# Products and last step of a long convolution in three channel parts instead of two, with a normalisation moved from VectorE to GpSimd and a new order table

## The chip, the cores and the metric

The kernel runs on one core of one Trainium2 chip. The time is the device time of the program in microseconds, from the runs of the unchanged kernel 651.96 us (median of three, 651.33 to 653.91). Five engines share the work: TensorE (PE, with its weight loads PEld), VectorE (DVE), ScalarE (ACT), GpSimd (POOL) and SyncE (SP), which here only issues transfers.

## The reference

Two independent layers over 2048 positions and 576 channels; their outputs are set side by side. All values are float32.

```python
# A: a state space layer as a long convolution, one filter K for each channel d
dt = exp(log_dt); A = -exp(log_A_real) + 1j * A_imag; C = (C_real + 1j * C_imag) * dt[:, None]
P = exp((A * dt[:, None])[:, :, None] * arange(L))          # [576, 128, 2048]
K = 2.0 * einsum("dn,dnl->dl", C, P).real                   # [576, 2048]
y = irfft(rfft(u_t, 2 * L) * rfft(K, 2 * L))[:, :, :L] + u * D_skip
# B: linear attention with a softmax feature map, 32 heads of 18 channels
q, k, v = split(x @ wqkv)
phi_q = concat([softmax(q @ w_phi), softmax(-(q @ w_phi))])  # per head
phi_k = concat([softmax(k @ w_phi), softmax(-(k @ w_phi))])
num = phi_q @ (phi_k^T v); den = phi_q . sum(phi_k) + 1e-6
b = (num / den) @ wo
out = concat([a, b], axis=-1)                                # [1, 2048, 1152]
```

## The kernel before

**Layer B** runs in sixteen key tiles and sixteen query tiles of 128 positions. A key tile (`key_tile`) loads x, splits it into a rounded and a rest part (`load_x`: one copy on ACT, two subtractions on POOL, L399), multiplies it by the folded key weights and the value weights, takes both softmaxes (`softmax`) and adds to one accumulated product of keys and values in PSUM. `softmax` takes maxima, minima and differences on DVE, a second difference on POOL, one exponential on ACT (L514), the sums and their reciprocals on DVE (L515, L516), and a product of the 128x1152 exponentials with the reciprocals on the engine that its argument names. For keys this is the constant `KN`, for queries "dve". The query tiles need all keys and the folded query weights, which take the place of the key weights in SBUF. Each query tile ends with its own store.

**Layer A** builds the filter in 36 groups of channels (`phases`, `waves`, `group`): phases on POOL (L793, L797), sines on ACT (L806 to L808), three small matmuls and exponentials in PSUM (L827), four products on DVE (L832 to L837), 32 small matmuls, and a copy to `ks`. Nine groups make a quarter of the channels, q = 0 to 3. At the end of a quarter `k_first` does the first step of its transform and writes it (L857) to `kd`, a scratch tensor in HBM. `u_first` does the same for u in sixteen pieces, and writes `ud` (L667). The transform's second step, the product with the filter and the way back are `product(p, half)`: eight blocks p of frequencies for each half of the channels. Such a unit loads the tables fu and fi (L895), four blocks ub of `ud` (L912), and for two rows r the table fk (L939) and a block kb of `kd` (L941). It runs 16 matmuls on ub, 8 on each kb and 16 back, each in two passes. In between ACT copies four tiles from PSUM to `us` and four to `zo`, DVE makes eight products `ac` and POOL four sums of them. Six stores (L978, L981) put the result into `zd`. Every read of `ud` waits for all of `ud`, every read of a `kd` tensor for all of that tensor; a half's `kd` is two quarters. `last(cb, half)` reads `zd` (L994), does the last step with eight matmuls, and stores half the channels of 256 positions (L1007).

**The order.** Nothing of this order is fixed by the loops. All operations are first collected with `pl.op`, each with an engine, an estimated cost and its operands. `Plan.run` then places them one by one: among the operations of an engine that could start now it takes the one with the smallest rank. The rank is the number that the table `WANT` gives to the unit that the operation belongs to (`pl.at("product", 3)` and so on). The same rank decides who gets a tile's buffers first: for most tiles a unit may not take a buffer ahead of a lower rank if that would leave the lower rank without one. So each engine's order of instructions, and SP's queue with it, comes out of this table and the estimated costs. Where the plan foresees PE waiting, `emit` puts filler matmuls on a tile of zeros (L200) ahead of an operation, so that PE keeps its clock.

Lines that the text names again: L200 the filler matmul, L388 every other matmul (`mm`), L393 and L395 copies, L399 every two-operand elementwise instruction (`tt`), L591 and L618 transposes of queries.

Of the kernel before, what the change touches and what calls it, by code (L numbers as in the profile page):

```python
# [26 lines left out]
HD = D // 2  # L27
BW = D // NB
# [306 lines left out]
def c_dma(nbytes, run=4096):  # L335
# [4 lines left out]
FR, KN = "dve", "dve"  # L340
# [29 lines left out]
def body(tc, nc, i, out, ctx):  # L370
    pl = Plan()
# [12 lines left out]
    tags({1: "gd", 5: "dram"}, space=DRAM)  # L384
# [252 lines left out]
    kd, zd = ([B("dram", [64, 64, HD]) for _ in range(2)] for _ in range(2))  # L637
# [212 lines left out]
    def k_first(qt, ks):  # L850
        def one(j):
# [3 lines left out]
            for c in range(2):  # L855
                b0, c0, d = 16 * j + 8 * c, qt % 2 * 4 * DQ, kd[qt // 2]
                op("sp", c_dma(64 * 4608, 576), lambda c=c, b0=b0, c0=c0, d=d: sp.dma_start(  # L857
                    d.t[:, b0:b0 + 8, c0:c0 + 4 * DQ], o.t[64 * c:64 * c + 64].rearrange("p b f d -> p b (f d)")), r=[o], w=[d])
# [30 lines left out]
    def product(p, half):  # L889

        pl.at("product", 8 * half + p)
        cs = halves[half]
        fu, fi = B("fu", [128, 4, 2, 32]), B("fi", [128, 2, 2, 64])
        for b, n in ((fu, "fu"), (fi, "fi")):
            op("sp", c_dma(128 * 1024, 1024), lambda b=b, n=n: sp.dma_start(b.t.rearrange("p a b c -> p (a b c)"), i[n][p]), r=[ud], w=[b])  # L895

        ub = [B("ub", [128, 2, HD]) for _ in range(2)]
# [6 lines left out]
        def take(par, r):  # L904
            q = 4 * p + 2 * r
            d = lambda: ub[par].t[64 * r:64 * r + 64]
            if par and not q:
                for j in range(2):
                    op("sp", c_dma(64 * 1152, 1152), lambda j=j: sp.dma_start(d()[:, j], block(1, j, ud)[:, cs]), r=[ud], w=[ub[1]])
                return  # L910
            a = 63 - q if par else q
            op("sp", c_dma(64 * 2304, 1152), lambda: sp.dma_start(  # L912
# [8 lines left out]
        us = [B("us2", [128, 2, HD]) for _ in range(2)]  # L921
        pu, begun = [B("ps", [128, HD]) for _ in range(4)], Mark()
# [8 lines left out]
        op("pe", 970, f, r=[fu, *ub], w=[*pu, begun], with_=us, mode=(64, 32))  # L931
        for r in range(2):
            for part in range(2):
                copy("act", lambda r=r, part=part: us[r].t[:, part], lambda r=r, part=part: pu[2 * r + part].t, [pu[2 * r + part]], [us[r]], HD)
        acs = []

        def times(r):
            fk, kb, ac = B("fk", [128, 2, 128]), B("kb", [128, 2, HD]), B("ac", [128, 4, HD])
            op("sp", c_dma(128 * 1024, 1024), lambda: sp.dma_start(fk.t.rearrange("p a b -> p (a b)"), i["fk"][2 * p + r]), r=[ud], w=[fk])  # L939
            blk = lambda: kd[half].t.rearrange("(p j r) b d -> p (r b) j d", j=2, r=2)[2 * p + r]  # L940
            op("sp", c_dma(128 * 2304, 1152), lambda: sp.dma_start(kb.t, blk()), r=[kd[half]], w=[kb])  # L941
            pk = [B("ps", [128, HD]) for _ in range(2)]
# [5 lines left out]
            op("pe", 970, f, r=[fk, kb, begun], w=pk, with_=[ac], mode=(128, 64))  # L948
            for part in range(2):
                for k, q in ((part, part), (2 + part, 1 - part)):  # L950
                    tt("dve", lambda k=k: ac.t[:, k], lambda q=q: us[r].t[:, q], lambda part=part: pk[part].t, ALU.mult, [us[r], pk[part]], [ac], HD)
# [5 lines left out]
            tt(YN[0], lambda: ac.t[:, 0], lambda: ac.t[:, 0], lambda: ac.t[:, 1], ALU.subtract, [ac], [ac], HD)  # L957
            tt(YN[1], lambda: ac.t[:, 2], lambda: ac.t[:, 2], lambda: ac.t[:, 3], ALU.add, [ac], [ac], HD)
# [3 lines left out]
        pz, zo = [B("ps", [128, HD]) for _ in range(4)], [B("zo", [128, 2, HD]) for _ in range(2)]  # L962
# [6 lines left out]
        op("pe", 970, back, r=[fi, *acs], w=pz, with_=zo, mode=(32, 64))  # L969
        for c in range(4):  # L970
            j, par = divmod(c, 2)
            copy("act", lambda c=c, j=j, par=par: zo[par].t[:, j], lambda c=c: pz[c].t, [pz[c]], [zo[par]], HD)

        def put(par, r):
            q = 4 * p + 2 * r
            s = lambda: zo[par].t[64 * r:64 * r + 64]
            if not par:
                op("sp", c_dma(64 * 2304, 1152), lambda: sp.dma_start(zd[half].t[q:q + 2].rearrange("j s d -> s j d"), s()), r=[zo[0]], w=[zd[half]])  # L978
# [57 lines left out]
```

## Time and profile before

| | us |
|---|---|
| median of three runs | 651.96 (651.33 to 653.91) |
| the profiled execution, its own time | 650.51 |
| span of its trace | 648.5 |

The mean granted TensorE clock is 0.982 of full speed. The transfer queue of SP has 101,574 packets, 102.81 MB, whose time is 55.6% of the span of 16 DMA engines. The trace's rows name engine, line, operation, out<-in with the shape, and a count; what follows is said where a row stands. A stage's row gives the time in which an engine was busy, its instructions in brackets, then the granted clock, the DMA share and GB/s. Matmuls are pipelined and their ends are modelled, so that a busy PE is not a PE at its peak, and the fillers count as busy.

### The profile page before, as it was taken

To read this page: it belongs to the slowest core of one execution; us is meant where nothing else is said; L and a number is where in the kernel's file an instruction comes from. 1 tells how busy PE (TensorE), PEld (TensorE's weight loads), DVE (VectorE), ACT (ScalarE), POOL (GpSimd) and SP (SyncE) were. 2 spreads that over 40 slices of the span, in tenths; PEclk is the share of its full clock that TensorE was granted. 3 is DMA by queue.
4 is the path that set the end of the run, shared out by engine and by line. 5 is a ranking of instruction groups with operands and counts; after the bars stand their busy time and mean duration, and the time that the engine had idled before them with its cause. 6 is when DMAs were issued, how large, how long until landed. Compare 5 with 4: busy or idle time off the path is not lost.

```text
span 648.5 us, 19206 instructions
## 1 busy us (share of the span) xinstructions
PE 597.5 (92%) x7782; PEld 468.8 (72%) x7782; DVE 468.5 (72%) x964; ACT 465.3 (72%) x838; POOL 298.3 (46%) x468
## 2 busy tenths in 40 slices
PE   9989999999998958978889999989979999999997
PEld 5878888888887836856666666656767876678885
DVE  6855978998986869964669787476795666657552
ACT  5799786999985968788778886889965354354332
POOL 1794646567724734560736745365301142435110
PEclk9989999999999979999979999898999999999999
DMA  8966432431256112355437866873567788897466
GB/s 220 290 221 197 128 127 76 136 100 47 67 127 171 33 36 75 99 118 187 144 98 194 230 162 188 226 201 81 167 187 183 222 240 221 227 259 182 149 199 203
DMA packets 101661, 104.02 MB, mean 160 GB/s; under 512 B 12358, under 2 KB 90054, under 8 KB 101574
## 3 DMA queue, kind: packets, MB, share of 16 engines
q1 hardware_dynamic: 101574, 102.81, 55.6%
q8 instruction: 61, 1.00, 0.7%
q14 instruction: 26, 0.21, 0.1%
HBM read 63.63 MB, written 39.06 MB: 158 GB/s over the span
## 4 chain that ended last, share of the span: by engine, by line
PE 43%; DVE 24%; ACT 15%; DMA 7%; issue 4%; POOL 4%; SPq 2%; POOLq 0%; ACTq 0%; DVEq 0%
PE ps L388 39%; DVE e L399 4%; DVE cs L832 3%; DVE E L833 3%; DMA xi<-in_xT_dram 2%; DVE small L515 2%; ACT cs L808 2%; ACT cs L806 2%; PE ps L591 2%; DMA ub<-dram 2%; ACT e L514 2%; ACT cs L807 2%; DVE E L835 1%; DVE E L837 1%; DVE small L516 1%
## 5 line engine op out<-in xcount | busy, mean ns | idle before, releaser
L388 PE MATMUL ps<-wh,xl 128*128 128x288 f32 (+2 forms) x448 | 141.2, 315 | 0.0
L388 PE MATMUL ps<-wh,xh 128*128 128x378 f32 (+2 forms) x400 | 134.7, 337 | 2.1 <-DVE E L833 1.1
L388 PE MATMUL ps<-wl,xh 128*128 128x378 f32 (+2 forms) x400 | 129.0, 323 | 0.0
L797 POOL TENSOR_TENSOR cs<-cs,pi 128x512 int32<-128x512 int32 (+4 forms) x180 | 112.7, 630 | 10.1
L388 PEld LDWEIGHTS ps<-wh,xh 128*128 128x128 f32 x400 | 76.0, 190 | 13.5 <-issue 5.2
L388 PEld LDWEIGHTS ps<-wh,xl 128*128 128x128 f32 x448 | 85.0, 190 | 0.5 <-DVE xl L399 0.3
L399 POOL TENSOR_TENSOR xl<-xi,xh 128x512 fp32r<-128x512 f32 x32 | 41.0, 1282 | 82.3 <-ACT xh L393 76.1
L388 PEld LDWEIGHTS ps<-wl,xh 128*128 128x128 f32 x400 | 75.9, 190 | 0.1
L399 POOL TENSOR_TENSOR ac<-ac 128x288 f32<-128x288 f32 x64 | 51.1, 822 | 46.1 <-DVE ac L399 45.0
L399 POOL TENSOR_TENSOR e<-small,e 128x576 f32<-128x576 f32 x32 | 38.3, 1195 | 72.8 <-DVE small L399 72.5
L832 DVE TENSOR_TENSOR cs<-ps,cs 128x1024 f32<-128x1024 f32 x36 | 43.9, 1218 | 25.7 <-ACT ps L827 25.5
L827 ACT ACTIVATE ps<-ps 128x512 f32<-128x512 f32 x108 | 56.4, 584 | 6.2 <-PE ps L388 5.7
L200 PE MATMUL ps<-zero 128*32 128x256 bf16 (+10 forms) x318 | 57.4, 319 | 1.2 <-DVE zero L415 1.2
L388 PE MATMUL ps<-E,cs 128*32 128x64 f32 x2304 | 44.2, 226 | 13.1 <-DVE E L835 9.6
L515 DVE TENSOR_REDUCE small<-e 128x64 f32<-128x1152 f32 x32 | 42.9, 1347 | 17.3 <-ACT e L514 17.2
L399 DVE TENSOR_TENSOR ac<-us,ps 128x288 f32<-128x288 f32 x128 | 48.9, 446 | 7.9 <-PE ps L388 4.2
L388 PEld LDWEIGHTS ps<-E,cs 128*32 128x32 f32 x2304 | 36.3, 113 | 24.4 <-DVE E L835 9.9
L388 PE MATMUL ps<-wh,xi 128*128 128x288 f32 x160 | 49.5, 311 | 1.0 <-DVE cs L832 0.7
L388 PEld LDWEIGHTS ps<-kvb,fT 126*128 126x128 f32 (+1 forms) x320 | 40.0, 195 | 14.0 <-ACT ks L393 4.5
L388 PE MATMUL ps<-kvb,fT 126*128 126x133 f32 (+1 forms) x320 | 42.7, 284 | 7.3 <-ACT ks L393 3.7
L506 DVE TENSOR_REDUCE small<-ps 128x16 f32<-128x288 f32 (+2 forms) x64 | 28.9, 452 | 26.3 <-PE ps L388 26.2
L388 PE MATMUL ps<-wl,xi 128*128 128x288 f32 x160 | 47.0, 295 | 0.0
(130 smaller groups left out, 1297.4 us busy)
## 6 DMA issues: line engine op xcount, KB each, us to landing
xi<-in_xT_dram SPq DMA_DIRECT2D x32, 320.0 KB
dram<-zi SPq DMA_DIRECT2D x16, 576.0 KB
dram<-zi SPq DMA_DIRECT2D x32, 288.0 KB
kb<-dram SPq DMA_DIRECT2D x32, 288.0 KB
zi<-dram SPq DMA_DIRECT2D x16, 576.0 KB
ub<-dram SPq DMA_DIRECT2D x62, 144.0 KB
ub<-in_u_dram SPq DMA_DIRECT2D x16, 288.0 KB
out_dram<-ot SPq DMA_DIRECT2D x16, 288.0 KB
```

What stands on the lines that cost most here:

```text
L200: self.matmul(t[0:cols, 0:n], self.zero.t[0:rows, 0:cols], self.zero.t[0:rows, 0:n])
L388: pe.matmul(o, l, r, start=start, stop=stop, skip_group_check=skip)
L399: op(eng, c_dve(n) if eng == "dve" else c_pool(n), lambda: e.tensor_tensor(dst(), a(), b(), op=alu), r=r, w=w, lock=eng == "pool" or not a ...
L506: op("dve", c_dve(DH * m), lambda: dve.tensor_reduce(mx.t, v(), axis=AX.X, op=ALU.max), r=[p], w=[mx])
L514: op("act", c_act(1152), lambda: act.activation(e.t, e.t, AF.Exp), r=[e], w=[e], table="exp")
L515: op("dve", 1270, lambda: dve.tensor_reduce(sm.t, e.t, axis=AX.X, op=ALU.add), r=[e], w=[sm])
L591: pe.transpose(tp.t[0:m, j - j0, :], e.t[:, sign, 7 * g:7 * g + GRP[g], :].rearrange("p h f -> p (h f)"), ident.t)
L797: op("pool", c_pool(2 * n * W), lambda n=n, j=j: pool.tensor_tensor(x()[:, :, :, n:2 * n], x()[:, :, :, 0:n], pi.t[:, j:j + 2, gs].bitcast ...
L806: act.activation(cs.t[:, 0], cs.t[:, 1].bitcast(I32), AF.Abs)
L827: op("act", c_act(512), lambda p=p: act.activation(p.t, p.t, AF.Exp), r=[p], w=[p], table="exp")
L832: op("dve", c_dve(64 * W), lambda: dve.tensor_tensor(F(), both(M.t), F(), op=ALU.mult), r=[M, cs], w=[cs])
L833: op("dve", c_dve(64 * W), lambda: dve.tensor_tensor(E.t[:, :, :, 32:64], both(up.t), cs.t[:, :, :, 0:32], op=ALU.mult), r=[up, cs], w=[E])
```

## The change

The channels of `product` and `last` are cut at 144 and 288 in place of 288 alone: `PARTS` has a quarter, a quarter and a half. There are three `kd` and three `zd` tensors. The filter's first two quarters each have their own, the last two share one. `product` runs for 24 units instead of 16, the first sixteen of them 144 columns wide. `last` still runs sixteen times with the same bytes; for a quarter part one run covers twice as many positions of half as many columns. The key tiles' normalisation goes from DVE to POOL (`KN`). `WANT` is replaced as a whole, with 24 ranks for `product`. Cut to its core:

```diff
+PARTS = ((0, D // 4), (D // 4, D // 2), (D // 2, D))
...
-FR, KN = "dve", "dve"
+FR, KN = "dve", "pool"
...
-    ident=[-265.4],
-    fold=[-386.9, -94.8, 140, 322.2],
-    start=[-91.6],
-    key=[-167.8, 70.6, 39.4, 134.7, 162.1, 26, -99.8, 92.7, 123.8, 136.5, 127.6, 52.4, 119.4, 85.3, 65.9, 81.6],
-    kv=[-232.9],
-    query=[857, 388.8, 625.9, 167.6, 333.7, 1000.1, 787.3, 438.6, 557.3, 379.6, 436.8, 493.6, 507.5, 170.5, 578,
-          1378.9],
-    u=[27, 41.2, 77.5, 103.4, 46.3, 50.8, 135.8, 91.1, 50, 111.5, 0.9, -22.5, 29.5, -53.6, -50.4, -78.3],
-    mags=[-26.4],
-    sel=[-18.9, 15.8],
-    dsk=[76.9],
-    par=[-542.3, 43.5, 82.6, 297.6, 159.4, 317.7],
-    group=[24.8, -7.3, 62.4, 23.8, 82, 75.2, 75.8, 64.7, 83.4, 149.4, 127.2, 124.6, 147.9, 105.6, 112.1, 89.2, 147.1,
-          147.3, 179.8, 174.3, 180.5, 158, 181.9, 162.3, 168.4, 199.5, 166.2, 403, 297.6, 505, 233.6, 353.9, 201.1,
-          483.7, 226.4, 210.4],
-    kfirst=[81.5, 102.8, 137.8, 237.5],
-    product=[224.1, 180.6, 177.4, 234.3, 183.8, 189.4, 217, 176.6, 337.3, 365.9, 305.8, 697.2, 383.1, 362.5, 442.5,
-          581.6],
-    last=[318.2, 194.4, 220.9, 233.7, 166.3, 179.1, 287.7, 234.6, 346.7, 612, 290.6, 373.2, 597.2, 1060.5, 389.3,
-          788.5],
+    ident=[158.3],
+    fold=[-399.2, -460.7, 208.1, 236.8],
+    start=[154.8],
+    key=[-397.9, 14.5, 186.8, 190.8, 14.1, -46.4, 46.9, 195, 140.8, -36.5, 189.4, 120.4, 27.6, 175.4, -333.1, 50.8],
+    kv=[-36.7],
+    query=[342.6, 1356.4, 1953, 830.4, 304.2, 281.8, 2222.6, 2128.9, 441.3, 305.2, 543.4, 2600.3, 387.2, 215.9, 436.8,
+          1162.7],
+    u=[43.7, -97.4, -36.7, -176.8, 8.4, -139.2, 72, 15.7, 88.3, -52.9, 95.1, 7.5, 25.4, -17.3, -306.4, -239.3],
+    mags=[-513.9],
+    sel=[-289, -179.6],
+    dsk=[-117.5],
+    par=[-1334.4, 78.7, 82.5, 238.7, 321.3, 330.9],
+    group=[-330.7, -34.3, -219, 24.6, -86.4, 29.4, 15.8, 11.2, -21.4, 112.1, 132.4, 87.4, 139.5, 110.1, 142, 116.9,
+          98, 124.6, 189.9, 182.7, 150.3, 191.9, 147.7, 205, 186.6, 171, 207.6, 364.8, 2555.3, 300, 420.5, 272.7,
+          516.6, 224.4, 307.1, 1435.8],
+    kfirst=[65, 107.4, 160.6, 341.3],
+    product=[323.1, 112.1, 99.9, 203.1, 190, 150.3, 357.2, 179, 307.7, 296.6, 335.2, 168.9, 158.7, 1560.5, 140.2, 251,
+          571.8, 401.9, 548.2, 1367.8, 555, 832.4, 590.8, 423.5],
+    last=[265.1, 257.9, 256.3, 373.4, 848.1, 1298.9, 525.5, 1353.4, 2098.2, 1503.9, 1536, 373, 984, 926.9, 1150.5,
+          407.5],
...
-    kd, zd = ([B("dram", [64, 64, HD]) for _ in range(2)] for _ in range(2))
+    kd, zd = ([B("dram", [64, 64, c1 - c0]) for c0, c1 in PARTS] for _ in range(2))
...
-                b0, c0, d = 16 * j + 8 * c, qt % 2 * 4 * DQ, kd[qt // 2]
+                b0, c0, d = 16 * j + 8 * c, max(0, qt - 2) * 4 * DQ, kd[min(qt, 2)]
...
-    def product(p, half):
-        pl.at("product", 8 * half + p)
-        cs = halves[half]
+    def product(p, part_of):
+        pl.at("product", 8 * part_of + p)
+        cs = slice(*PARTS[part_of])
+        wd = cs.stop - cs.start
...
-        op("pe", 970, f, r=[fu, *ub], w=[*pu, begun], with_=us, mode=(64, 32))
+        op("pe", 3.37 * wd + 20, f, r=[fu, *ub], w=[*pu, begun], with_=us, mode=(64, 32))
...
-    def last(cb, half):
-        pl.at("last", 8 * half + cb // 4)
-        yo, zi = B("yo", [128, 2, HD]), B("zi", [128, 4, HD])
+    def last(k, part_of, cb):
+        pl.at("last", k)
+        c0, c1 = PARTS[part_of]
+        n = c1 - c0
+        m = HD // n
+        yo, zi = B("yo", [128, 2, HD]), B("zi", [128, 4 * m, n])
         op("sp", c_dma(128 * 4608), lambda: sp.dma_start(
-            zi.t, zd[half].t.rearrange("q (r b) d -> (q r) b d", r=2)[:, cb:cb + 4]), r=[zd[half]], w=[zi])
+            zi.t, zd[part_of].t.rearrange("q (r b) d -> (q r) b d", r=2)[:, cb:cb + 4 * m]), r=[zd[part_of]], w=[zi])
...
+    k = 0
+    for part_of, (c0, c1) in enumerate(PARTS):
+        m = HD // (c1 - c0)
+        for cb in range(0, 32, 4 * m):
+            last(k, part_of, cb)
+            k += 1
```

The other lines of the diff put the width `wd` in place of 288 in the shapes, costs and transfers of `product`.

More of the change, by code (lines that the diff above doesn't have):

```diff
@@ L383, in body @@
     tags({8: "ps"}, space=PSUM, window=1000)
-    tags({1: "gd", 5: "dram"}, space=DRAM)
+    tags({1: "gd", 7: "dram"}, space=DRAM)
     B, op = pl.buf, pl.op
@@ L920, in place @@
             return 1 - j if par and (p or r) else j
-        us = [B("us2", [128, 2, HD]) for _ in range(2)]
-        pu, begun = [B("ps", [128, HD]) for _ in range(4)], Mark()
+        us = [B("us2", [128, 2, wd]) for _ in range(2)]
+        pu, begun = [B("ps", [128, wd]) for _ in range(4)], Mark()
         def f():
@@ L961, in product @@
             times(r)
-        pz, zo = [B("ps", [128, HD]) for _ in range(4)], [B("zo", [128, 2, HD]) for _ in range(2)]
+        pz, zo = [B("ps", [128, wd]) for _ in range(4)], [B("zo", [128, 2, wd]) for _ in range(2)]
         def back():
@@ L1004, in last @@
             copy("act" if r else "dve", lambda r=r: yo.t[:, r], lambda r=r: ps[r].t, [ps[r]], [yo], HD)
-        for n in range(2):
+        for h in range(2):
             st = out.ap[0][0]
-            op("sp", c_dma(64 * 2304, 1152), lambda n=n: sp.dma_start(bass.AP(
-                tensor=out.tensor, offset=out.offset + (2 * n + cb) * st + HD * half, ap=[[32 * st, 64], [st, 2], [1, HD]]),
-                yo.t[64 * n:64 * n + 64]), r=[yo])
-    for half in range(2):
-        for cb in range(0, 32, 4):
-            last(cb, half)
+            op("sp", c_dma(64 * 2304, 4 * n), lambda h=h: sp.dma_start(bass.AP(
+                tensor=out.tensor, offset=out.offset + (2 * m * h + cb) * st + c0, ap=[[32 * st, 64], [st, 2 * m], [1, n]]),
+                yo.t[64 * h:64 * h + 64].rearrange("p r (b d) -> p (r b) d", b=m)), r=[yo])
+    k = 0
[4 more added lines that the diff above has]
+            k += 1
     with tc.manual_schedule():
```

45 lines of the change are left out of this document (23 added, 22 removed).

## The prediction

> **What bounds the kernel now.** I read the page's head first, then the busy time of the engines in four stages (cut at the first key softmax, the end of the keys, and the two ends of the products), then the filler matmuls in the same stages, then the transfers that open and close each stage.
>
> ```profile
> span 648.5 us, 19206 instructions
> PE 597.5 (92%) x7782; PEld 468.8 (72%) x7782; DVE 468.5 (72%) x964; ACT 465.3 (72%) x838; POOL 298.3 (46%) x468
> PE 43%; DVE 24%; ACT 15%; DMA 7%; issue 4%; POOL 4%; SPq 2%; POOLq 0%; ACTq 0%; DVEq 0%
> ...
> 33.00:200.00 167.00, 162.10 (x2418) 140.72 (x2417) 138.02 (x265) 145.28 (x240) 99.83 (x157) 0.99 0.42 126
> 200.00:300.00 100.00, 81.54 (x1113) 65.45 (x1111) 74.12 (x154) 78.42 (x127) 50.60 (x80) 0.97 0.34 94
> 300.00:505.00 205.00, 186.87 (x2726) 134.49 (x2726) 147.54 (x277) 164.33 (x302) 91.48 (x153) 0.97 0.61 170
> 505.00:648.50 143.50, 135.83 (x1355) 104.75 (x1353) 84.64 (x202) 56.71 (x134) 42.00 (x50) 1.00 0.75 213
> ```
>
> In a stage's row the busy columns are PE, its weight loads, DVE, ACT and POOL; then come granted clock, DMA share and GB/s. PE carries the largest share of the chain of waits and is the fullest engine in every stage. But part of its busy time is filler on zeros, which L200 issues where the plan foresees a gap. The same stages for the zero tile alone (first column again PE):
>
> ```profile
> 200.00:300.00 100.00, 19.29 (x132) 12.96 (x132) 0.00 (x0) 0.97 0.34 94
> 300.00:505.00 205.00, 12.60 (x69) 6.39 (x69) 0.00 (x0) 0.97 0.61 170
> 505.00:648.50 143.50, 11.58 (x54) 5.58 (x54) 0.00 (x0) 1.00 0.75 213
> ```
>
> So PE does nothing useful for 100 − 81.54 + 19.29 = 37.8 us of the 100 us after the keys, for 205 − 186.87 + 12.60 = 30.7 us of the next 205, and for 7.7 + 11.6 = 19.3 us of the last 143.5. Between 33 and 200 us it idles 4.9 us of 167: that stage is full. The hole to look at is 200 to 300 us. What could have been run there shows in the transfers that go through the scratch tensors in HBM:
>
> ```profile
> L981 SPq DMA_DIRECT2D dram<-zo x64: 540/595/1939, 344.4 to 606.0; - x64
> L912 SPq DMA_DIRECT2D ub<-dram x62: 573/610/1699, 314.8 to 582.3; - x62
> L857 SPq DMA_DIRECT2D dram<-zi x32: 574/634/2056, 178.1 to 506.4; - x32
> L941 SPq DMA_DIRECT2D kb<-dram x32: 371/450/1217, 294.9 to 589.3; - x32
> L667 SPq DMA_DIRECT2D dram<-zi x16: 320/327/583, 28.7 to 306.1; - x16
> ```
>
> The first quarter's filter leaves at 178 us (L857, first), but the first product starts at 295 to 315 us (L941, L912): it needs a half, that is two quarters, and also all sixteen pieces of u, whose last is written only at 306 us (L667). The last filter quarter leaves by 506 us, the last product result at 606 us.
>
> **The quarter units: cost of the split.** Eight units of half a width become sixteen of a quarter: the same columns, with twice the instructions. One half unit's matmuls, from the timeline (start, duration; the last row holds both rows r of one kind):
>
> ```profile
> 521.70 1.20 PE L388 MATMUL ps<-ub,fu 64*32 64x288 f32 x32
> 524.88 1.23 PE L388 MATMUL ps<-ac,fi 32*64 32x288 f32 x32
> 526.62 2.16 PE L388 MATMUL ps<-kb,fk 128*64 128x288 f32 x16
> ...
> L388 PE MATMUL ps<-kb,fk 128*64 128x288 f32 x256 | 38.4, 433 | 2.0 <-ACT xi L393 1.1 <-DVE E L833 0.5 <-DMA kb<-dram 0.3
> L591 PE MATMUL ps<-ident,e 128*126 128x128 f32 x128 | 17.8, 279 | 7.0 <-DVE e L399 6.4 <-DVE cs L832 0.6
> ```
>
> A half unit is 1.20 + 1.23 + 2.16 = 4.59 us of PE. No 144-column matmul is in the trace; between the 279 ns of 128 columns and the 433 ns of 288, a straight line gives 279 + 16/160 × 154 = 294 ns, 0.68 of the half's. So I take 0.68 × 4.59 = 3.1 us a quarter unit, 16 × 3.1 = 50 us in place of 8 × 4.59 = 36.7: +13.2 us. The bounds are 0 (time goes with the columns) and +36.7 (a quarter unit as long as a half).
>
> ```profile
> L393 ACT ACTIVATE us<-ps 128x288 f32<-128x288 f32 x64 | 22.3, 418 | 22.5 <-PE ps L388 20.0 <-issue 2.0
> L393 ACT ACTIVATE v<-ps 128x396 f32<-128x396 f32 x16 | 8.1, 506 | 5.0 <-PE ps L388 4.9
> L393 ACT ACTIVATE v<-ps 128x180 f32<-128x180 f32 x16 | 5.2, 325 | 5.3 <-PE ps L388 2.3 <-DVE small L507 1.5 <-DVE small L399 0.9
> L399 DVE TENSOR_TENSOR ac<-us,ps 128x288 f32<-128x288 f32 x128 | 48.9, 446 | 7.9 <-PE ps L388 4.2 <-ACT zo L393 3.5
> L399 DVE TENSOR_TENSOR e<-ps,small 128x198 f32<-128x198 f32 x16 | 5.6, 351 | 0.4 <-ACT v L393 0.4
> L399 POOL TENSOR_TENSOR ac<-ac 128x288 f32<-128x288 f32 x64 | 51.1, 822 | 46.1 <-DVE ac L399 45.0 <-PE ps L388 1.1
> L399 POOL TENSOR_TENSOR e<-small,e 128x576 f32<-128x576 f32 x32 | 38.3, 1195 | 72.8 <-DVE small L399 72.5
> L399 DVE TENSOR_TENSOR e<-e,small 128x1152 f32<-128x1152 f32 x32 | 46.0, 1440 | 0.4
> ```
>
> ACT: (506 − 325)/216 = 0.84 ns an element, so 295 ns at 144; two for one cost 590 − 418 = 172 ns, times 64 copies of the eight units, +11.0 us. DVE: (446 − 351)/90 = 1.06 ns, so 294 ns; (588 − 446) × 64 = +9.1 us. POOL: (1195 − 822)/288 = 1.30 ns, so 635 ns; (1270 − 822) × 32 = +14.3 us. Each of the three has 0 as its lower bound and the full second instruction as its upper one (26.8, 28.5 and 26.3 us). POOL idles more than half of 200 to 505 us and covers its share; DVE and ACT are settled with the hole below.
>
> **Transfers and the SP queue.** Eight more units issue 16 transfers each (2 of fu and fi, 4 of ub, 2 of fk, 2 of kb, 6 of zo). At the 450 to 610 ns of the rows above that is 128 × about 0.55 = 70 us more of SP's queue, spread over 200 to 505 us; behind them in that queue stand the x loads of the queries and the parameter loads. The bytes of ub, kb and zo stay, in runs of 576 B in place of 1152 B (144 and 288 columns of four bytes); new are fu, fi and both fk of eight units:
>
> ```profile
> zi<-dram SPq DMA_DIRECT2D x16, 576.0 KB
> kb<-dram SPq DMA_DIRECT2D x32, 288.0 KB
> ub<-dram SPq DMA_DIRECT2D x62, 144.0 KB
> dram<-zo SPq DMA_DIRECT2D x32, 144.0 KB
> dram<-zo SPq DMA_DIRECT2D x64, 72.0 KB
> out_dram<-yo SPq DMA_DIRECT2D x32, 144.0 KB
> fk<-in_fk_dram SPq DMA_DIRECT2D x32, 128.0 KB
> fu<-in_fu_dram SPq DMA_DIRECT2D x16, 128.0 KB
> ```
>
> fi has fu's size, so 8 × 4 × 128 KB = 4.1 MB. The stages 200 to 300 and 300 to 505 us have DMA shares of 0.34 and 0.61, so I cost this at nothing. Without that cover it is 4.1 MB at 213 GB/s = 19 us, the upper bound.
>
> **The key normalisation on POOL.** Sixteen products leave DVE: 16 × 1.44 = −23 us there. POOL does not show 1152 elements; twice its 576-element row is 2.39 us, the straight line from the 288 and 576 rows gives 1.94. I take 2.39, since the operands are alike: +38 us on POOL, whose 33 to 200 us go from 99.8 to 138 of 167. DVE's relief falls in the stage where PE idles 4.9 us, so I give it nothing (bound: −4.9 us). The wait it adds: on POOL the phase steps of the next groups (L797) and the x remainders queue behind the product, and ACT's sines and PE's key matmuls wait for those. The 67 us that POOL idles in this stage hide it; were that gone, each key would pay 2.39 − 1.44 = 0.95 us, 15 us in all (upper bound).
>
> A row speaks against putting work of two SBUF operands on POOL beside DVE. At the start of the keys the two ran into each other:
>
> ```profile
> 37.99 1.93 DVE L399 TENSOR_TENSOR e<-e,small 128x1152 f32<-128x1152 f32 x1
> ...
> 38.68 1.33 POOL L793 COPY cs<-pi 128x32 int32<-128x32 int32 x1
> ...
> L399 DVE TENSOR_TENSOR e<-e,small x32: 1341/1358/2144, 38.0 to 628.4; 128x1152 f32<-128x1152 f32 x32
> ```
>
> The product took 1.93 us in place of its median of 1.36, and the small copy behind it ended with it. The Trainium skill, page "SBUF — State Buffer", section "SBUF: two separate sides", makes this a lock: GpSimd and a VectorE instruction with two SBUF inputs exclude each other for a whole instruction. The trace agrees in this one place (0.57 us lost). By that rule in its worst form the sum gets 38 us more (16 × 2.39, an estimate from the rule). By the rows it gets nothing that can be seen: mean and median of DVE's product over the whole kernel differ by 0.08 us.
>
> **The sum.** Quarter 0 is half of the first half's products: 18.4 us of PE leaves the time after 300 us. In the hole it needs 8 × 3.1 = 25.0 us of PE out of 37.8 free, 64 × 0.295 = 18.9 us of ACT out of 21.6 free, and 64 × 0.294 = 18.8 us of DVE out of 25.9 free. All three fit, ACT barely; u must be finished some 100 us earlier, and the new table gives every u piece 95.1 or less where the old one went to 135.8. So −18.4 us (bounds 0 and −18.4). Quarter 1 runs in 300 to 505 us and pays its half of the split there, +6.6 us (0 to +18.4). The profiled execution took 650.5 us, 2.0 beside its span: 650.5 − 18.4 + 6.6 = 638.7. The median of the runs, 651.96, stands 1.5 above that execution, so 640.
>
> **The rivals.** *The tail sets the end.* The last filter quarter needs groups 27 to 35, and the new table ranks group 28 at 2555.3 and group 35 at 1435.8, behind nearly everything; the half part cannot start before them. Behind it stand eight half units of 576 (ub) + 576 (kb) + 576 (zo) + 512 (tables) KB and eight last steps of 576 + 288 KB, 24.8 MB. At the 213 GB/s of the last stage that is 117 us; from 506 to 648.5 us there are 142. So a delay of the last filter quarter beyond about 25 us decides, and each further microsecond is one of the total: a delay of 35 us gives 662. Against it: two rank values are not times, and ACT and DVE have room for two groups. *The port.* Each of the sixteen normalisations holds DVE for its 2.39 us, as the product above was held for 0.57: 38 us, of which DVE's 29 us of idle time in the key stage take half, 652 + 19 = 671. Against it speak the 0.08 us. This is what the lock of that page would do at its worst. *Nothing gained.* The hole's work is given back: groups come later by as much as ACT spent on quarter 0, and 300 to 505 us, where ACT is busy 164 of 205, lengthens by 18.9 less the 18.4: 652. For it: in the hole ACT would be at 97%. *Much more.* The new order also removes half of the other 50 us of idle and filler after 300 us: 640 − 25 = 615. Against it: the last stage's transfers already run at 0.75. *The split doesn't come early:* if quarter 0 is still run after 300 us, only the split's cost is left, +13.2: 665.
>
> **How the numbers follow.** Forecast 0.40, much more 0.17, nothing gained 0.13, the tail 0.19, the port 0.05, not early 0.06. Within 0.5% (3.3 us, about what a measurement can tell from no change) lies nearly all of "nothing gained"; faster are the forecast's and the larger gain, slower the last three. That gives 0.57, 0.12 and 0.31. The forecast's own range is 633 to 648: from a split that costs quarter 1 nothing to the edge of what can be told. To leave out 2 in 10 it must reach most of the larger gain and of the tail: 616 to 667.
>
> **What would show it.** Right: the first kb load near 200 us, u's last write before it, filler plus idle of PE in 200 to 300 us down from 37.8 to some 15 us, 144-column matmuls near 294 ns, 16 normalisations on POOL near 2.4 us. Wrong: the last filter write later than 530 us with a last stage bound by transfers; DVE instructions stretched beside POOL's; ACT full and the groups later, with new filler in 300 to 505 us.

## The result, and the profile after

| | median, us | runs | ratio to before (95%) |
|---|---|---|---|
| before, same chip | 652.67 | 651.33 to 653.91 | |
| after | 685.54 | 683.64 to 687.17 | 1.0503 (1.0467 to 1.0539) |

The change makes the kernel 32.9 us slower. The forecast was 640.0, the range ended at 667. The head of the page of after: span, busy time of the engines, shares of the chain of waits.

```profile
span 684.0 us, 20992 instructions
...
PE 624.6 (91%) x8445; PEld 495.7 (72%) x8445; DVE 468.6 (69%) x1015; ACT 477.7 (70%) x908; POOL 329.1 (48%) x516
...
PE 55%; ACT 16%; DVE 11%; DMA 8%; issue 4%; SPq 3%; POOL 2%; POOLq 0%; DVEq 0%; ACTq 0%
```

DVE is busy as long as before (468.5), ACT 12 us longer, POOL 31 us longer; none of the three comes near its upper bound in the prediction. PE is busy 27.1 us longer and idle 684.0 − 624.6 = 59.4 us in place of 51.0. The stages of after from the end of the keys on, cut where its last filter write leaves (524 us in place of 505), with the columns of the prediction; the second block is the zero tile alone.

```profile
200.00:300.00 100.00, 83.62 (x1242) 65.04 (x1239) 76.78 (x150) 82.56 (x145) 57.42 (x93) 0.85 0.45 121
300.00:524.00 224.00, 197.60 (x3121) 156.33 (x3120) 146.46 (x331) 171.68 (x339) 93.79 (x172) 0.93 0.50 138
524.00:684.00 160.00, 150.92 (x1513) 115.21 (x1511) 91.79 (x223) 60.46 (x145) 44.94 (x55) 1.00 0.74 215
```

```profile
200.00:300.00 100.00, 13.67 (x87) 8.34 (x87) 0.00 (x0) 0.85 0.45 121
300.00:524.00 224.00, 18.98 (x114) 9.58 (x113) 0.00 (x0) 0.93 0.50 138
524.00:684.00 160.00, 11.47 (x60) 5.59 (x60) 0.00 (x0) 1.00 0.74 215
```

Three things stand here. In 200 to 300 us idle and filler fell only from 37.8 to 100 − 83.62 + 13.67 = 30.1 us, and the granted clock is 0.85 in place of 0.97. The middle stage is 19 us longer, and idle and filler in it rose from 30.7 to 224 − 197.60 + 18.98 = 45.4 us, at a clock of 0.93 and a DMA share of 0.50 in place of 0.61: fewer bytes a second, yet more waiting. The last stage is 16.5 us longer, but not starved: idle and filler are 20.6 us against 19.3; it has 150.92 − 11.47 = 139.5 us of real PE work left, where before had 124.3.

The transfers through the scratch tensors (smallest, median and longest time on SP's queue in ns, first and last start in us):

```profile
L983 SPq DMA_DIRECT2D dram<-zo x96: 445/595/1564, 234.3 to 631.1; - x96
L914 SPq DMA_DIRECT2D ub<-dram x93: 585/607/1607, 213.0 to 617.6; - x93
L943 SPq DMA_DIRECT2D kb<-dram x48: 359/384/1398, 194.3 to 619.5; - x48
L980 SPq DMA_DIRECT2D dram<-zo x48: 595/602/1762, 231.8 to 628.5; - x48
L858 SPq DMA_DIRECT2D dram<-zi x32: 445/594/1576, 172.1 to 523.8; - x32
L668 SPq DMA_DIRECT2D dram<-zi x16: 326/327/629, 35.1 to 206.1; - x16
```

Of before, the row of zo's other stores, beside the ones that the prediction shows:

```profile
L978 SPq DMA_DIRECT2D dram<-zo x32: 589/599/1902, 343.1 to 603.4; - x32
```

Quarter 0 does start early: the first kb load is at 194 us in place of 295, and u is finished at 206 in place of 306. But only a part of it runs early. The instructions on the tile `ac` between 200 and 300 us (PE, its weight loads, DVE, ACT, POOL, then clock, DMA share and GB/s):

```profile
200.00:300.00 100.00, 2.70 (x64) 1.98 (x64) 3.58 (x16) 0.00 (x0) 4.86 (x8) 0.85 0.45 121
```

A unit has 32 matmuls on `ac`. So two of the eight units of quarter 0 are done in the hole; the other six come after 300 us.

And a transfer of half the bytes takes the queue as long as a whole one did: 595 to 610 ns for zo and ub in both kernels (the rows of after mix both widths; taken apart, they differ by 4 ns at most). The zo, ub and kb rows hold 285 transfers, 160.9 us of the queue by count times median, against 190 transfers and 109.5 us in the same four rows of before. What that looks like in the middle stage, from the timeline of SP's queue in after (start, duration):

```profile
331.11 1.26 SPq L980 DMA_DIRECT2D dram<-zo  x2
332.43 2.51 SPq L983 DMA_DIRECT2D dram<-zo  x4
334.98 0.58 SPq L941 DMA_DIRECT2D fk<-in_fk_dram  x1
335.67 0.38 SPq L943 DMA_DIRECT2D kb<-dram  x1
336.15 0.41 SPq L897 DMA_DIRECT2D fu<-in_fu_dram  x1
336.61 0.42 SPq L897 DMA_DIRECT2D fi<-in_fi_dram  x1
337.08 2.58 SPq L914 DMA_DIRECT2D ub<-dram  x4
339.71 1.41 SPq L941 DMA_DIRECT2D fk<-in_fk_dram  x1
```

From 331.1 to 341.1 us there is hardly a gap: the stores of one unit, then the loads of the next, one behind the other.

The instructions of the quarter units (x count, then busy us and mean ns), and below them the matmuls that are still 288 wide:

```profile
L400 POOL TENSOR_TENSOR e<-e,small 128x1152 f32<-128x1152 f32 x16 | 34.5, 2162 | 1.6 <-ACT ps L828 1.1 <-DVE small L517 0.3
...
L400 DVE TENSOR_TENSOR ac<-us,ps 128x144 f32<-128x144 f32 x128 | 29.4, 295 | 23.9 <-PE ps L389 13.5 <-ACT us L394 7.4 <-ACT zo L394 2.8
L389 PE MATMUL ps<-kb,fk 128*64 128x144 f32 x256 | 24.0, 320 | 5.4 <-DMA kb<-dram 1.8 <-ACT ps L828 1.4 <-ACT zo L394 1.3
...
L389 PE MATMUL ps<-ub,fu 64*32 64x144 f32 x512 | 18.5, 319 | 2.3 <-DVE E L834 0.8 <-DVE cs L833 0.6 <-DVE o L400 0.4
L389 PE MATMUL ps<-ac,fi 32*64 32x144 f32 x512 | 15.2, 314 | 3.1 <-DVE xl L400 2.3 <-POOL ac L400 0.8
L394 ACT ACTIVATE us<-ps 128x144 f32<-128x144 f32 x64 | 14.1, 292 | 6.4 <-PE ps L389 6.2
```

```profile
L389 PE MATMUL ps<-kb,fk 128*64 128x288 f32 x128 | 17.7, 413 | 0.8 <-DMA kb<-dram 0.4 <-ACT zo L394 0.3
L389 PE MATMUL ps<-ub,fu 64*32 64x288 f32 x256 | 14.1, 409 | 1.0 <-DMA ub<-dram 0.6
L389 PE MATMUL ps<-ac,fi 32*64 32x288 f32 x256 | 9.9, 415 | 0.0
```

Sixteen quarter units take 24.0 + 18.5 + 15.2 = 57.7 us of PE; eight half units in the same kernel take 41.7. By these rows the split costs PE about 57.7 − 41.7 = 16 us. Fifteen of the sixteen quarter units ran in the stages with a clock of 0.85 and 0.93, the half units at 1.00, so that this difference holds more than the split.

Last, the start, from the timeline of PE in after and then in before:

```profile
17.28 2.44 PE L389 MATMUL ps<-fT,e 126*128 126x126 f32 x20
...
25.09 0.48 PE L389 MATMUL ps<-wh,xh 128*128 128x396 f32 x1
```

```profile
7.83 3.73 PE L388 MATMUL ps<-fT,e 126*128 126x126 f32 x30 [0.20 <-DMA e<-in_wkT_dram]
...
16.25 0.47 PE L388 MATMUL ps<-wh,xh 128*128 128x378 f32 x1
```

The new table puts the loads for the magnitudes and the value weights ahead of the fold's, 60 fillers stand ahead of the fold's matmuls in place of 16, and the keys begin 8.8 us later.

### The profile page after: what moved, and what is told of

Same layout as the page of the kernel before. It is cut to its first block, busy times and chain, and to the rows that moved or that the text cites. A ratio compares the mean times of both kernels' runs of the same rounds, so it can differ in the third digit from the quotient of the medians.

```text
span 684.0 us, 20992 instructions
## 1 busy us (share of the span) xinstructions
PE 624.6 (91%) x8445; PEld 495.7 (72%) x8445; DVE 468.6 (69%) x1015; ACT 477.7 (70%) x908; POOL 329.1 (48%) x516
## 4 chain that ended last, share of the span: by engine, by line
PE 55%; ACT 16%; DVE 11%; DMA 8%; issue 4%; SPq 3%; POOL 2%; POOLq 0%; DVEq 0%; ACTq 0%
PE ps L389 49%; PE ps L592 2%; PE ps L201 2%; ACT cs L807 2%; ACT cs L809 2%; DVE ac L400 2%; ACT ps L828 2%; DMA xi<-in_xT_dram 2%; ACT cs L808 2%; DMA E<-in_wkT_dram 1%; ACT L808 1%; ACT L828 1%; DVE small L516 1%; DVE cs L833 1%; DMA kb<-dram 1%
## 5 line engine op out<-in xcount | busy, mean ns | idle before, releaser
L389 PE MATMUL ps<-wh,xl 128*128 128x288 f32 (+2 forms) x448 | 144.3, 322 | 1.4 <-POOL xl L400 1.4
L798 POOL TENSOR_TENSOR cs<-cs,pi 128x32 int32<-128x32 int32 (+4 forms) x180 | 108.2, 603 | 9.7
L400 POOL TENSOR_TENSOR ac<-ac 128x144 f32<-128x144 f32 (+1 forms) x96 | 57.3, 619 | 86.7 <-DVE ac L400 78.0
L389 PEld LDWEIGHTS ps<-wh,xl 128*128 128x128 f32 x448 | 87.6, 196 | 2.2 <-POOL xl L400 2.2
L201 PE MATMUL ps<-zero 128*128 128x504 bf16 (+14 forms) x341 | 63.6, 325 | 8.5 <-ACT zi L654 2.4
L400 DVE TENSOR_TENSOR ac<-us,ps 128x144 f32<-128x144 f32 (+1 forms) x192 | 53.5, 345 | 23.9 <-PE ps L389 13.5
L828 ACT ACTIVATE ps<-ps 128x512 f32<-128x512 f32 x108 | 57.7, 589 | 4.8 <-PE ps L389 4.4
L507 DVE TENSOR_REDUCE small<-ps 128x21 f32<-128x378 f32 (+1 forms) x64 | 28.7, 449 | 44.8 <-PE ps L389 44.3
L201 PEld LDWEIGHTS <-zero 128*128 128x128 bf16 (+6 forms) x341 | 32.0, 106 | 32.4 <-issue 18.2
L389 PE MATMUL ps<-wl,xi 128*128 128x288 f32 x160 | 49.0, 308 | 0.0
L515 ACT ACTIVATE e<-e 128x1152 f32<-128x1152 f32 x32 | 37.2, 1171 | 15.2 <-POOL e L400 15.2
```

Of the source, the lines that this page charges most:

```text
L201: self.matmul(t[0:cols, 0:n], self.zero.t[0:rows, 0:cols], self.zero.t[0:rows, 0:n])
L389: pe.matmul(o, l, r, start=start, stop=stop, skip_group_check=skip)
L400: op(eng, c_dve(n) if eng == "dve" else c_pool(n), lambda: e.tensor_tensor(dst(), a(), b(), op=alu), r=r, w=w, lock=eng == "pool" or not a ...
L507: op("dve", c_dve(DH * m), lambda: dve.tensor_reduce(mx.t, v(), axis=AX.X, op=ALU.max), r=[p], w=[mx])
L515: op("act", c_act(1152), lambda: act.activation(e.t, e.t, AF.Exp), r=[e], w=[e], table="exp")
L798: op("pool", c_pool(2 * n * W), lambda n=n, j=j: pool.tensor_tensor(x()[:, :, :, n:2 * n], x()[:, :, :, 0:n], pi.t[:, j:j + 2, gs].bitcast ...
```

## The experiments

The theory after this reading: SP's queue, which in the timeline above takes one transfer behind the other, is the price; every transfer added holds it for some 0.6 us, loads come late behind stores, and PE waits. The rivals: the normalisation on POOL holds DVE; the split's arithmetic costs more than its PE time; the late start; or the new order as such. Each run's ratio is to before on the same chip.

**The normalisation alone, in both directions.** The order of before or after is kept, only the engine that executes the sixteen products differs.

```diff
-    def tt(eng, dst, a, b, alu, r, w, n):
-        e = dve if eng == "dve" else pool
+    def tt(eng, dst, a, b, alu, r, w, n, on=None):
+        e = on or (dve if eng == "dve" else pool)
...
-        e = softmax([(pa, slice(0, 21), lambda: by_head(pa.t)), (pb, slice(21, 32), lambda: by_head(pb.t[:, 0:198]))], KN)
+        e = softmax([(pa, slice(0, 21), lambda: by_head(pa.t)), (pb, slice(21, 32), lambda: by_head(pb.t[:, 0:198]))], KN, on=pool)
```

Before with the products on POOL:

> The kernel before, with its own order of instructions on every engine; only the sixteen key normalisations are executed by POOL where that order has them for DVE. Port theory (the loss comes from POOL's work beside DVE): DVE's small two-operand instructions of the key stage are held up and the time rises by 15 to 20 us, to 668 to 673. Order theory (the loss comes from the new table's order) and split theory (from the eight additional units): within 4 us of 652.7.

Measured: 653.86 against 653.55, ratio 1.0018 (0.9986 to 1.0050). After with the products back on DVE:

> The changed kernel in its own order; only the key normalisations go back to DVE, at the places where they stood for POOL. Port theory: 15 to 20 us less, 665 to 671. Order and split theory: within 4 us of 685.5; the stretched small instructions of DVE (412 ns in place of 223 for 21 elements) go back, but the keys end no earlier.

Measured: 688.40, ratio 1.0555 (1.0492 to 1.0619), no better than after. From the groups by shape of before, then of before with the products on POOL:

```profile
L399 DVE TENSOR_TENSOR small<-small 128x21 f32<-128x21 f32 x16 | 3.6, 223 | 0.0
```

```profile
L399 POOL TENSOR_TENSOR e<-e,small 128x1152 f32<-128x1152 f32 x16 | 34.4, 2154 | 1.6 <-DVE small L516 1.4
...
L399 DVE TENSOR_TENSOR small<-small 128x21 f32<-128x21 f32 x16 | 6.8, 425 | 0.0
```

DVE's small products beside POOL's stretch from 223 to 425 ns. The Trainium skill, page "SBUF — State Buffer", section "SBUF: two separate sides", expects such waiting between a GpSimd instruction and a VectorE one with two SBUF inputs. The trace agrees that the second is stretched, by 202 ns a time in the mean; the kernel's time doesn't show it. The port rival falls.

**The split at the order of before.** Eight units of before do everything twice on 144 columns; plan and order stay.

```diff
+        two = (slice(0, HD),) if half else (slice(0, HD // 2), slice(HD // 2, HD))
...
+        def each(fn):
+            return lambda: [fn(s) for s in two]
...
-            op("sp", c_dma(128 * 2304, 1152), lambda: sp.dma_start(kb.t, blk()), r=[kd[half]], w=[kb])
+            op("sp", c_dma(128 * 2304, 1152), each(lambda s: sp.dma_start(kb.t[:, :, s], blk()[:, :, s])), r=[kd[half]], w=[kb])
```

The transfers of ub and zo, the matmuls, copies, products and sums likewise.

> The kernel before in its own order; each of the eight units of its first half executes its matmuls, copies, products, sums and transfers of ub, kb and zo twice, on 144 columns each time (the tables are loaded once). Split theory: the +15 us of PE that the changed kernel's rows show are paid in full, 664 to 668. Order theory: PE has idle and filler in that stage, so half of it or less, 653 to 660. Port theory: 652.7.

Measured: 695.28, ratio 1.0662 (1.0591 to 1.0734), +41.7 us: more than the whole loss of after, and far above the 16 us that the rows give for PE.

**Another order of the unsplit work.** The plan's cost of the products' matmuls is 990 in place of 970, which is enough for it to order the work differently.

```diff
-        op("pe", 970, f, r=[fu, *ub], w=[*pu, begun], with_=us, mode=(64, 32))
+        op("pe", 990, f, r=[fu, *ub], w=[*pu, begun], with_=us, mode=(64, 32))
```

> The kernel before with the same table, the same instructions and the same widths; only the plan's estimate for the product's matmuls is 990 in place of 970, as it is for a half in the changed kernel, which gives another order of the same work. Order theory: an order that was not chosen for exactly these estimates costs 10 to 30 us, 663 to 683. Split and port theory: 652.7, within 3 us.

Measured: 673.93, ratio 1.0346 (1.0283 to 1.0409), +20.4 us with the same work, and 98 fillers more (PE has 7880 matmuls in place of 7782). An order alone moves this kernel by 3%, so only runs at one fixed order can price a part. The next runs keep to that.

**Arithmetic and transfers apart.** First only the matmuls, copies, products and sums are cut in two, then only the transfers of ub, kb and zo (96 more, the same bytes, runs of 576 B).

> The kernel before in its own order; only the matmuls, copies, products and sums of its first eight units are executed twice on 144 columns; their transfers stay whole. Engine theory (of the 41.7 us that the full split cost, PE, ACT, DVE and POOL pay most): 675 to 690. Queue theory (SP's queue, where each transfer takes about 0.6 us to issue, pays most): 655 to 668, of which up to 15 us are PE's longer matmuls.

Measured: 661.15 against 652.18, ratio 1.0131 (1.0094 to 1.0168), +9.0 us.

> The kernel before in its own order; only the transfers of ub, kb and zo of its first eight units are issued twice, with half the columns each (576 B runs, the same bytes); matmuls and elementwise work stay whole. Queue theory: 12 more issues in each of eight units, about 57 us of queue in a stage where the queue is issuing 70 to 90% of the time; 20 to 35 us more, 673 to 690. Engine theory: within 5 us of 653.5.

Measured: 688.81, ratio 1.0556 (1.0506 to 1.0606), +36.6 us, 0.38 us for each of 96. Together the two make 45.6, near the 41.7 of both at once, and the arithmetic is the small part. What PE waited for in before, then in the kernel with cut transfers (us in total, times, the longest):

```profile
PE ps L388 <- DMA kb<-dram: 0.3, 1, 0.3
```

```profile
PE ps L388 <- DMA ub<-dram: 9.9, 7, 5.7
...
PE ps L388 <- DMA kb<-dram: 3.5, 4, 1.4
```

So the loads of ub and kb do come late. Added up from its timeline, SP's queue is issuing for 0.77 of the time from 300 to 505 us, in before for 0.58. The middle stage of the kernel with cut transfers:

```profile
300.00:505.00 205.00, 167.55 (x2201) 114.13 (x2201) 120.21 (x223) 139.87 (x253) 85.59 (x149) 0.88 0.50 136
```

PE is busy 167.6 us in place of 186.9 and the clock granted is 0.88 in place of 0.97, while the DMA share falls from 0.61 to 0.50: all engines do less, the DMA engines too. Over the whole run the same matmuls keep PE busy longer, which the head of its page shows:

```profile
PE 617.2 (89%) x7781; PEld 479.5 (69%) x7782; DVE 468.9 (68%) x964; ACT 466.6 (68%) x838; POOL 296.5 (43%) x468
```

Of its span's 690.4 − 648.5 = 41.9 us, PE idles 22.2 and is busy 19.7 longer on the 7782 matmuls of before. Its mean clock is 0.946 against 0.982. So this run pays twice, in waiting and in a lower clock; why the clock falls is not shown.

**Number of transfers or length of their runs?** The same 96 more transfers, but each cut by partitions, so that a run stays 1152 B.

```diff
+        cut = lambda n: (slice(0, n),) if half else (slice(0, n // 2), slice(n // 2, n))
...
-            op("sp", c_dma(128 * 2304, 1152), lambda: sp.dma_start(kb.t, blk()), r=[kd[half]], w=[kb])
+            op("sp", c_dma(128 * 2304, 1152), lambda: [sp.dma_start(kb.t[s], blk()[s]) for s in cut(128)], r=[kd[half]], w=[kb])
```

> The order of before, with the transfers of ub, kb and zo of its first eight units again cut in two, but by partitions instead of columns: 96 more transfers as in the run with cut transfers, the same bytes, and every contiguous run still 1152 B. If the number of issues through SP's queue is the price, it comes out as that run did: 680 to 692 us (+28 to +40, about 0.38 us for each of 96). If the short runs of 576 B were the price, nothing is left: 649 to 656 us. Between the two, say 665, both have a part.

Measured: 674.29 against 651.95, ratio 1.0349 (1.0285 to 1.0412), +22.3 us: between the two. The queue's price of a transfer shows why; first the kernel cut by columns, then the one cut by rows.

```profile
L994 SPq DMA_DIRECT2D dram<-zo x96: 540/595/1620, 353.4 to 647.9; - x96
L920 SPq DMA_DIRECT2D ub<-dram x93: 573/606/1487, 318.4 to 624.7; - x93
```

```profile
L982 SPq DMA_DIRECT2D dram<-zo x96: 365/422/2056, 346.5 to 628.2; - x96
L913 SPq DMA_DIRECT2D ub<-dram x93: 335/430/1435, 316.1 to 604.4; - x93
L942 SPq DMA_DIRECT2D kb<-dram x48: 368/580/2130, 296.3 to 611.2; - x48
```

With half the columns a transfer holds SP for 595 to 606 ns, as long as whole; with half the rows for 422 to 430. In these patterns the price goes with the partitions that a transfer spans, and neither with its bytes nor with the number of its runs: in before, stores of 64 partitions take 595 ns with one run for each partition (L981), 599 with two (L978) and 634 with eight (L857). It is not in proportion to the partitions: kb's loads of 128 took 450 ns in before, and those cut to 64 by rows take longer, which lifts the row's median to 580. Cutting by columns, as the change does, leaves the partitions as they are and so doubles the queue's time for the same bytes.

Added up from the timelines, SP's queue is held for 298 us in before, 357 in the kernel cut by columns and 331 in the one cut by rows: 59 us more for +36.6, and 33 us more for +22.3, some two thirds of the added queue time in both. The smaller price of the cut by rows needs no second cause.

**Fewer transfers, other things equal.** In both kernels the two stores of a row in the mirrored half (L981) become one, by having ACT's copies put the two blocks in mirrored order in `zo`. The plan is left as it is.

```diff
-            copy("act", lambda c=c, j=j, par=par: zo[par].t[:, j], lambda c=c: pz[c].t, [pz[c]], [zo[par]], wd)
+            copy("act", lambda c=c, j=1 - j if par and p else j, par=par: zo[par].t[:, j], lambda c=c: pz[c].t, [pz[c]], [zo[par]], wd)
...
+                def one(j):
+                    if not p:
+                        sp.dma_start(block(1, 2 * r + j, zd[part_of]), s()[:, j])
+                    elif not j:
+                        sp.dma_start(zd[part_of].t[63 - q:65 - q].rearrange("j s d -> s j d"), s())
```

After, with 42 transfers fewer:

> The changed kernel in its own order; in units p of 1 to 7 the two stores of zo's second tile become one (ACT's copies put the two blocks the other way round): 42 issues fewer, some 25 us of SP's queue, the same bytes. Queue theory: 6 to 15 us less, 670 to 680. Engine theory: within 4 us of 685.5.

Measured: 672.86 on a chip where before had 652.18, ratio 1.0318 (1.0281 to 1.0356); 12.7 us less than after, 0.30 us a transfer. Its mean clock is 0.974 where after has 0.952, and PE's busy time 610.4 us where after has 624.6; PE's idle time, 668.7 − 610.4 = 58.3 us, is almost that of after. In after the profile puts only 3.1 us of PE's idle time down to loads of kb and ub (2.2 and 0.9). So that the queue is the price in after rests on this run and on those at the order of before, and with the merged stores 20.7 us of its loss are still left. Before, with 28 fewer:

> The kernel before in its own order with the same merged stores: 28 issues fewer, some 17 us of SP's queue. Queue theory: 2 to 8 us less than the kernel before, since its queue is nearly full only from 340 to 420 us. Engine theory: within 3 us.

Measured: 646.69 against 652.18, ratio 0.9908 (0.9878 to 0.9938). This is faster than both kernels of the case. The merged store holds the queue 597 ns in after and 602 in before, as long as one of the two did.

**The transfers on another queue.** The Trainium skill, page "Perfetto Trace Analysis", section "DMA Optimizations", suggests spreading transfers over the engines that can issue them when issuing is the bottleneck. In the kernel of before with merged stores, ACT issues the 48 writes of the two first steps (`dram<-zi`) behind its own copies, in place of SP; in a second run the 68 stores of zo too.

```diff
-                op("sp", c_dma(64 * 4608, 576), lambda c=c, b0=b0, c0=c0, d=d: sp.dma_start(
+                op("sp", c_dma(64 * 4608, 576), lambda c=c, b0=b0, c0=c0, d=d: act.dma_start(
```

> Before with the merged zo stores, and the 48 writes of the filter's and u's first step (dram<-zi) issued from ACT's queue, behind ACT's own copies that made them, instead of SP's. Queue theory: 48 issues of about 0.6 us less on SP, 32 of them between 178 and 506 us, beside the merged kernel's 646.7: 637 to 643 us. Rival, that ACT pays the issue itself (48 x 0.6 = 29 us, in stages where ACT is busy four fifths of the time): 655 to 676.

Measured: 658.05 against 651.95, ratio 1.0093 (1.0056 to 1.0129).

> As the run with the 48 writes on ACT's queue, and the merged zo stores (68) on ACT's queue too. Queue theory: SP loses 68 more issues, mostly between 344 and 606 us: 630 to 641 us. Rival, ACT pays 116 x 0.6 = 70 us, in the stage from 300 to 505 us where it has 41 us free: 665 to 700.

Measured: 668.73, ratio 1.0251 (1.0200 to 1.0302). Two rows of the second run:

```profile
L978 ACTq DMA_DIRECT2D dram<-zo x32: 582/596/1126, 353.8 to 620.9; - x32
L984 ACTq DMA_DIRECT2D dram<-zo x28: 582/604/1926, 355.2 to 622.2; - x28
```

A transfer takes ACT 596 to 604 ns, as it took SP, and ACT has copies, sines and exponentials behind it. Against the merged kernel's 646.7 the 48 cost 11 us, the 116 cost 22. PE's idle time that the profile puts down to ACT rises from 11.1 us in the merged kernel to 19.3 in the second run. The suggestion did not help with this engine in this kernel. The writes stand in ACT's order where the plan had put them for SP; a plan that reckons with them on ACT was not tried.

**The late start.** In after, the fold's loads and work were put back to the front, first together with the work of other engines:

```diff
...
+        return rest[:22] + loads[:5] + x + late + work[:24] + rest[22:40] + loads[5:] + work[24:] + rest[40:]
```

> The order of after, except that the fold's first loads go ahead of the mags and value weights and the fold's work ahead of the later preparation, as in before. Theory that the late start (first real matmul 17.3 against 7.8 us) is passed on to the end: 676 to 681 us (-5 to -9.5). Rival, that SP's queue after 300 us sets the end anyway and takes the head start in: 683 to 688.

Measured: 699.25, ratio 1.0719 (1.0663 to 1.0776), 13.7 us slower than after. Then on SP alone, with 16 fillers in place of 60:

```diff
+        f = [x for x in sp if unit(x[0]) == ("fold", 0)][:5]
+        x = [x for x in sp if unit(x[0])[0] == "key"][:1]
...
+        for k, nf in rest[:at] + f + x + rest[at:]:
+            if len(done) < 1 and self.ops[k][0] == "pe":
+                nf = 16
+                done.append(k)
+            yield k, nf
```

> The order of after on every engine but SP; there the five loads of the fold and one load of x go ahead of the loads for mags and value weights, and 16 fillers in place of 60 stand ahead of the fold's first matmuls. First real matmul near 8 us, first key matmul some 5 to 9 us earlier than 25.1. If the late start is passed on: 676 to 681 us against after's 685.5 (-5 to -9). If it is taken up later: 683 to 688. Slower than 690 would mean that the mags, now loaded later, held the groups.

Measured: 699.05 against 653.58, ratio 1.0694 (1.0638 to 1.0750). Neither run does what was meant, and the timeline of PE in the second says why:

```profile
8.29 2.85 PE L411 MATMUL ps<-fT,e 126*128 126x126 f32 x20
...
27.11 0.70 PE L411 MATMUL ps<-fT,kvb 72*128 72x72 f32 x2 [13.61 <-DVE wl L470]
...
32.47 0.48 PE L411 MATMUL ps<-wh,xh 128*128 128x396 f32 x1
```

The fold starts 9 us earlier, but DVE's roundings of its weights stand in DVE's order behind the magnitudes, whose loads are now later; the first key matmul comes at 32.5 us in place of 25.1. With the merged stores as well:

> The same head together with the merged stores of the earlier run (672.9). If the two prices are separate and both are passed on: 663 to 668 us, still above before. If one hides the other: 671 to 674.

Measured: 678.67, ratio 1.0386 (1.0341 to 1.0432): no better than the merged kernel alone (1.0318). A clean delay is the kernel of before with 60 fillers ahead of its fold and nothing else:

```diff
+            if nf and not late:
+                nf, late = 60, True
             self.emit(k, o, nf)
```

> The order of before on every engine, with one difference: 60 fillers in place of 16 ahead of the first matmuls of the fold, so that the first real matmul starts at about 17 to 19 us instead of 7.8, as in after. If a late start is passed on to the end, 661 to 664 us (+9 to +12). If it is taken up later (SP's queue or a table load has slack to give), 651 to 656 us.

Measured: 658.68 against 653.58, ratio 1.0100 (1.0048 to 1.0153), +5.1 us. From its PE timeline and its transfers:

```profile
15.75 3.51 PE L390 MATMUL ps<-fT,e 126*128 126x126 f32 x30
```

```profile
L983 SPq DMA_DIRECT2D dram<-zo x64: 540/595/1407, 351.4 to 611.6; - x64
...
L943 SPq DMA_DIRECT2D kb<-dram x32: 367/486/1387, 302.0 to 593.3; - x32
```

A start 7.9 us later puts the first kb load 7.1 us later, the last product store 5.6, and the end 5.1. There is little slack to absorb a late start. After's 8.8 us later keys are worth some 5 to 6 us by this, an estimate (5.1 × 8.8 / 7.9); the interval of the run reaches from 3 to 10 us.

## Why the prediction was wrong

**The step that failed** is the one on the transfers and SP's queue: "70 us more of SP's queue, spread over 200 to 505 us", followed by "I cost this at nothing". The amount was right: added up from the timelines, SP issues 631 transfers in 362 us, before 502 in 298, so 129 transfers and 63 us more. The price was wrong. The cover that I named was the DMA share, 0.34 and 0.61, which measures the DMA engines and not the queue in front of them; my upper bound, 19 us, was by bytes for the same reason. At a fixed order the cut transfers alone cost 36.6 us, with no more bytes, and PE waited 13.4 us for ub and kb in place of 0.3. I had written down that the x loads stand behind the new transfers in that queue, and did not ask for the queue's own occupancy in the stage: 0.58 from 300 to 505 us in before, 0.71 in after. The 32 more table loads of after were in none of the runs at the order of before, so that their part is not measured.

**The split's arithmetic.** Forecast +13.2 us of PE, half of it on the path. PE's rows in after give about 16, since a 144-column matmul took 314 to 320 ns there and not 294. In the run with the arithmetic alone it took 290 to 311, and the eight split units took 46.7 us of PE against 38.2 for the eight whole ones, 8.5 more; the run cost 9.0, which holds PE, ACT, DVE and POOL together. The term was somewhat large for PE and near what the time showed. ACT's and DVE's rows in after show 292 and 295 ns for 144 columns, where 295 and 294 were forecast.

**The hole.** Forecast −18.4 us. The three signs came out in part: the first kb load at 194 us was near the 200 named, u's last write at 206 came after and not before it, and idle and filler in 200 to 300 us fell by 7.7 us and not to 15. This step failed too: the −18.4 needs all eight units of quarter 0 in the hole, and two were run there, worth 2 × 2.3 = 4.6 us at the prediction's price. PE had 30 us of idle and filler left for the others, so room on PE was not what was missing. The two are as many as have ranks below every unit of quarter 1 in the new table (99.9 and 112.1); the next rank, 140.2, is a unit of quarter 1, whose filter is written at 282 to 295 us, and the next kb load comes at 300 us. That fits, but no run tests it.

A rough account: 36.6 (transfers) + 9.0 (arithmetic) + 5 to 6 (start) is 51, less 4.6 for the two units is some 46, and after lost 32.9. The 13 us between are not explained; the new order is in them, and a run with another order moved 20 us by itself.

**The normalisation.** Costed at nothing, and that was right in both directions (1.0018, and no gain in putting it back). POOL's product took 2.16 us against the 2.39 I had taken.

**The rivals.** The tail did not decide: the last filter write left at 523.8 us, 17 us later, under the 25 from which I let it count, and the last stage has no more waiting than before. "Nothing gained" was nearest to the mechanism, since the middle stage gave back more than the hole gained, but it named ACT, whose share in that hole was 0.83 and not 0.97. None of the rivals had SP's queue as its mechanism, so that nothing in the range carried its price. The start was in none of them either, though the new ranks of the fold and the magnitudes stood in the diff.

## What to carry to other kernels

Look at the occupancy of the issuing queue in the stage that a change touches, not only at the share of the DMA engines: cutting a tile along its contiguous axis kept the bytes and doubled the queue's time for them here. Merging two stores that differ only in the order of their rows is the cheapest edit of this case, worth 5.5 us in one kernel and 12.7 in the other. When an order is made by a plan, price a part by doing it at the old order; otherwise 3% of reordering covers it.

## What the runs showed of the hardware

- A transfer of 64 partitions holds the issuing queue as long with 144 columns as with 288 (595 to 610 ns), nearly as long with one run for each partition as with eight (595 and 634 ns), with half the partitions 422 to 430 ns, and ACT's queue as long as SP's (596 to 604 ns). Those of 128 partitions took less than those of 64: 327 ns (u's writes) and 450 (kb). Why is not shown.
- Two kernels with the same 7782 matmuls kept PE busy 597.5 and 617.2 us, at mean granted clocks of 0.982 and 0.946: with the cut transfers came 22.2 us of idle time and 19.7 us of slower work. What lowers the clock in a given stage stays open, since 200 to 300 us had 0.97 in before and 0.85 in after, with less idle time in after.
- What stays open too: whether 576 B runs cost the DMA engines something beside the queue's time. Keeping the number of transfers and shortening the runs alone was not tried.
